# Clustered attention feeding a SoLU layer: the first batch's last pairs loaded in 3072-byte pieces, and w_out's column sums as fp32 products on PE

## The chip, the cores and the metric

The kernel runs on one core of one Trainium2 chip. A core has five engines with a queue of instructions each, taken in order: PE (TensorE, matrix products into PSUM), DVE (VectorE), ACT (ScalarE), POOL (GpSimd) and SP (SyncE, which here issues most of the transfers between HBM and the on-chip memory SBUF; 16 DMA engines carry them out). The metric is the device time of one execution in microseconds (us); lower is better.

## The reference

Attention comes first, for 4 batches, 8 heads, 768 tokens and a head dimension of 64, then a feed-forward layer over the 3072 tokens of 512 values:

```python
q_n = q / (norm(q) + 1e-6); k_n = k / (norm(k) + 1e-6); c_n = centroids / (norm(centroids) + 1e-6)
q_assign = argmax(einsum('bhsd,hcd->bhsc', q_n, c_n))          # 16 clusters a head
k_assign = argmax(einsum('bhsd,hcd->bhsc', k_n, c_n))
mask = q_assign[:, :, :, None] == k_assign[:, :, None, :]
scores = where(mask, (q @ k.T) / sqrt(64), -1e9)
attn = softmax(scores) @ v
x = attn, tokens by heads*64                                     # 3072 x 512
h = x @ w_in                                                     # 512 x 1024
solu = h * softmax(h)
ln = (solu - mean(solu)) / sqrt(var(solu) + 1e-6) * g_ln
out = ln @ w_out                                                 # 1024 x 512
```

A query sees only the keys of its own cluster. A norm of q or k does not change its argmax, so the kernel leaves it out.

## The kernel before

**Tiling.** Work goes by pairs of heads: four batches of four pairs, written (b, p), with names such as `ld0.3.1` for batch 0, pair 3, tensor 1 (0 is q, 1 is k). For each pair q and k are needed with the head dimension on the partitions. Batch 0 is loaded token by token (`load_tokens`, L353): a partition holds six tokens, and each of the two heads of the pair is a transfer of its own (192 KB, pieces of 64 fp32 values, 256 bytes, since the two heads lie side by side in SBUF). PE turns such a tile in six fp32 transposes of 128x128 (`tp`, L359) into a bank of the three-bank PSUM region `hreg`, and DVE or ACT copies it to `xt` (`xa`, L366). Pair (0,0) is done in two halves of the sequence. Batches 1 to 3 are loaded in pieces of 128 bytes and turned on DVE (`xt`, L384).

**Clusters.** From `xt` come two things. Casts (`ca`, L395) write bf16 copies into `qk`, k scaled by 1/256. A cluster group (`cl`, L407) multiplies `xt` with the centroids in fp32: four products with 32 output columns each stand side by side on PE (`tile_position`), one for each half of q and of k, over 384 tokens; the table `c_bd` has the centroids of the pair's two heads in 16 columns each, zero for the other head's rows. DVE then turns the result (`tb`), takes the maximum (`mx`), compares (`oh`) and turns it back (`ot`); four copies (`pl`, L450) place the one-hot rows below the 64 rows of q and k in `qk`, so that a score product over 80 or 96 rows adds the mask, and `bl` (L467) blanks the other head's rows for the second head.

**Attention.** `S` (L539) fills a bank of scores, two products of 256 columns in most units (one of 384 in pair (0,0), four of 128 in the last two pairs). `E` (L545) is ACT's exponential of a bank, `V` (L562) six value products of 65 columns, the last of them the sum of weights, and `N` (L587) the division on DVE. A ring of three score banks and one of nine exponential tiles tie S, E and V together. There are 294 banks: 24 of pair (0,0), 18 of every other pair.

**Feed-forward.** For each of 24 tiles of 128 tokens: x is turned by a transposing DMA (`tx`, on SP), `h` (L648) is eight products of 512 columns into hreg, then the maximum (`hm`), the exponential (`ex`, on ACT), the product (`u`), the statistics (`bn`, `ag`), another transposing DMA (`tu`), `y` (L709), eight products with w_out, and the scaling (`sc`) and store (`ou`). The mean is taken out of w_out beforehand: `sum_w_out` (`su`, L512) adds up the eight row blocks of w_out times g on DVE, one instruction a block, `me` (L521) sums that over the partitions with one fp32 product, and `ce` (L524) writes the centred bf16 weights.

**Order.** The program lists every step with its needs and then emits them in an order that is written out by hand for each engine (`ORDER`, from L28: a kind and how many of it in a row). `AWAY` (from L73) says which steps go to another engine than their usual one. A planner's costs, keys and due times stand beside each step (`add`), but the order written out decides. Since every queue is taken in order, an instruction that waits holds all that stand behind it on its engine.

The steps that the prediction speaks of are `ld` and `lo` (w_out's load) on SP, `tp`, `cl`, `S`, `V`, `me` on PE, `xa`, `ca`, the assignment steps `tb mx oh ot`, `pl`, `bl`, `N`, `su`, `ce` on DVE, and `E`, `ex` on ACT.

Of the kernel before, what the change touches and what calls it, by code (L numbers as in the profile page):

```python
# [22 lines left out]
class Weave:  # L23
# [6 lines left out]
        ld4 lv si ld11 lo lg ld lo lv ld2 lo ld3 lo ld2 lv ld3 lv ld3 li ld3 li2 ld2 li ld3 tx ld3  # L30
        lv ld3 lv ld5 tx2 lv tu ld3 tu ld lv ld9 tu ld4 lv ld6 tu2 ou2 tx lv ld3 tx ld tu ld ou lv
        tu ld6 ou ld7 tx ld5 ou ld2 lv ld2 ou ld6 ou tu ld4 tu2 lv ld pl2 tx ld2 ou ld lv2 tx lv pl
        tu2 pl tx ou2 pl3 tu2 ou tu ou tx2 tu ou tu tx tu ou tx tu ou tx ou2 tu ou tu2 ou6
    """
    ORDER["POOL"] = """
        po ca2 pl2 ca bl pl2 bl sg cv ca3 pl ca pl4 ca z bl z2 cv pl3 ca cv ca pl ca bl ca cv ca pl2
        ca pl cv pl ca cv ca cv pl2 ca wi pl wi z pl wi2 pl2 ca bl2 cv pl2 ca2 cv pl2 cv ca3 pl at z
        ca cv ca pl3 bl2 al at cv ca2 cv2 al pl ca pl ca at cv at ca3 pl3 al pl al ca6 at bl pl cv
        ca al pl3 cv2 at pl al ca2 bl ca pl2 at bl cv al pl ca at ca2 cv pl cv pl2 al pl at ca cv bl
        pl2 ca2 bl at ca3 al ca2 at cv at cv ca4 cv ca pl3 cv bl at pl al pl bl at al pl al at2 ca  # L40
        al pl cv at al2 at al3 at3 al2 at2 al2 at al2
    """
    ORDER["PE"] = """
        wm tp2 cp tp cl tp fl5 cl fl5 S3 tp S tp S2 tp2 S3 tp2 cl V tp2 V2 S3 cl S2 V3 S tp2 S2 gt
        S2 tp S2 V3 S2 tp S3 V S V S V S2 cl S3 V3 S2 V S2 V S V S4 V2 S V S2 V2 S2 V S2 me S2 V S
        V3 S2 V2 S3 cl S2 V S2 V2 S V2 S V S4 V S V3 S3 cl S3 V2 S V2 S3 V S2 V3 S2 h S h S2 h2 S3
        cl S V2 S V2 h V2 S h S2 h S h S2 V S V3 S V S V S h2 cl S2 h S h S2 V S V2 S h S2 V3 S2 y4
        S2 V2 S V2 S2 h V2 S2 h2 S2 y S V2 S y3 S3 V h2 S h S V h S V2 S2 h2 S2 V S V cl V2 S2 h V2
        S3 cl S2 V3 S2 V h S2 y S V2 S V2 S y S2 y2 h V S2 V h2 S V S h S2 h y S2 V y3 S2 V2 S h S
        V2 S V S h2 S2 V S cl h S V3 S2 h y V y S y S2 y V2 S h2 S3 V h V S y S y3 V3 h S V S2 y S y  # L50
        S2 V2 y S2 y S h V2 S2 h S V2 S2 cl S3 V2 cl h S2 V S V2 S h2 V S2 h S h S2 V cl V3 S2 V S y
        V y S3 y h S y V S V2 S2 y S V h S2 h S V2 S V2 S2 y2 S3 h2 V2 y S V2 S2 h3 S3 V h S V cl S2
        V2 S V cl S V S2 h S h V S V S y3 S2 V h V2 y S V S2 h S h S h S V2 S V S y2 h S y V2 y S V
        h S h3 S3 h V2 S2 V y S y2 V y V2 S2 h3 S3 V h y2 V y V S y V S3 h2 S V S V S y S V2 y S3 y2
        h2 S V h2 S3 h V y S V2 y3 S h S2 h V2 h S y S V2 y2 h S y S h V h S h S V S y V2 y S y S y
        h4 y4 h S h y4 S h2 V4 y3 ptx y h2 y h2 ptu2 y8 ptu2 y7
    """
    ORDER["DVE"] = """
        cn cb ca tb mx oh ot pl2 cv tb mx oh ot xa3 ca2 tb ca xa pl mx oh tb ot xa gk N su xa2 mx su
        oh xa ot N tb su3 mx N oh su3 N ot xt2 ce N ce bl xt tb mx oh ot N ce xt N ce4 tb N mx oh ot  # L60
        ce xt N xt hm tb mx u N oh ot hm xt2 u tb N mx oh hm bn2 ag bn ot N u xt bn N bn2 hm ag xt u
        bn xt hm N ag xt u tb cv bn N ag mx oh tb ot N mx hm oh N xt u bn3 hm ot bn N ag2 u bn2 xt
        ag hm N tb xt mx oh ot u N hm xt2 bn ca bn ag N xt u bn xt sc bn hm N tb mx oh ot u tb mx N
        xt hm oh tb N ot u xt mx N oh ag hm bn3 N xt u N ag ot hm xt2 tb mx u N tb oh mx hm bn2 ot u
        bn N bn2 hm oh ot ag cv ag u N bn hm bl ag u bn cv N bn cv hm bn2 u N ag sc hm bn ag bn ag N
        bn u sc hm N u ag sc bn2 hm N bn u bn ag bn ag hm N u bn ag bn hm sc u bn2 sc ag hm N bn tx
        u bn2 hm tu ag tu ag u bn2 ag sc
    """
    ORDER["ACT"] = """
        wa xa4 ca3 E6 xa E3 xa3 E78 ex E10 ex E14 ex E5 sc E6 ex E4 sc E4 ex E17 ex E sc E7 ex E6 sc  # L70
        E5 ca E3 ex E4 sc E4 ex E sc E14 ex E12 ex E7 sc E10 ex E6 sc E4 ex E9 ex E7 sc E3 ex E3 sc
        E3 ex E2 sc E5 ex E9 ex E5 ex E8 ex E sc E4 ex sc E ex E3 ex sc ex sc2 tu2 sc2 oz
# [3 lines left out]
        ca0.0.0.0.1 ca0.0.0.1.0 ca2.2.1.0 tu23.1 xa0.0.0.1 xa0.0.1.0 xa0.1.1.0 xa0.2.0.0 xa0.2.0.1  # L76
        xa0.2.1.1
    """.split(), "ACT"))
    AWAY.update(dict.fromkeys("""
        bl0.3 bl3.3 ca0.0.0.0.0 ca0.0.1.1.1 ca0.1.1.0 ca0.2.0.0 ca3.0.0.0 cv0.0.1 cv1.3.1 cv3.1.1  # L80
        cv3.2.1 cv3.3.0 pl0.0.0.0.1 pl0.0.0.1.1 pl0.0.1.0.1 sc12 sc13 sc14 sc17 sc18 sc6 tu22.0
    """.split(), "DVE"))
    AWAY.update(dict.fromkeys("""
        ca0.0.1.0.1 ca0.0.1.1.0 pl0.0.0.0.0 pl0.0.0.1.0 pl0.0.1.0.0 pl0.0.1.1.0 pl0.1.0.0 pl0.1.0.1
        pl0.1.1.0 pl0.1.1.1 pl0.2.0.0 pl0.2.0.1 pl0.2.1.0 pl0.2.1.1 pl0.3.0.0 pl0.3.0.1 pl0.3.1.0
        pl0.3.1.1 pl1.0.0.0 pl1.0.0.1 pl1.0.1.0 pl1.0.1.1 pl1.1.0.0 pl1.1.0.1 pl1.1.1.0 pl1.1.1.1
        pl1.2.0.0 pl1.2.0.1 pl1.2.1.0 pl1.2.1.1 pl1.3.0.0 pl1.3.0.1 pl1.3.1.0 pl1.3.1.1 pl2.0.0.0
        pl2.0.0.1 pl2.0.1.0 pl2.0.1.1 pl2.1.0.0 pl2.1.0.1 pl2.1.1.0 pl2.1.1.1 pl2.2.0.0 pl2.2.0.1
        pl2.2.1.0 pl2.2.1.1 pl2.3.0.0 pl2.3.0.1 pl2.3.1.0 pl2.3.1.1 pl3.0.0.0 pl3.0.1.1 pl3.1.0.0
        pl3.1.0.1 pl3.1.1.1 pl3.2.0.0 pl3.2.1.0 pl3.3.0.0 pl3.3.1.0  # L90
# [79 lines left out]
def kernel(  # L170
# [172 lines left out]
    def by_token(b):  # L343

        return b < n_turned

    def halves_of(b, p):
        return (b, p) == (0, 0)
# [9 lines left out]

    def turn_tokens(b, p, i, hf):  # L359

        j = tps[b, p, i, hf]
        for t in range(n_t // 2):
            uses(nc.tensor.transpose(hreg[:, j, t * P:(t + 1) * P],  # L363
                                     tokens(b, p, i)[:, hf * (n_t // 2) + t, :], ident_f[:]), j)
# [29 lines left out]

    def cast(b, p, i, hh, cols, e):  # L395
        xt, h = xts[b, p, i], 2 * p + hh
        r = rows(h)
        dst = side(b, p, i, hh, cols)[:D]
        if e == "ACT":
            nc.scalar.activation(dst, xt[r, cols], Act.Copy, scale=inv_C if i else 1.0)  # L400
        elif i == 0:
            VEC[e].tensor_copy(dst, xt[r, cols])  # L402
        else:
            VEC[e].tensor_scalar(dst, xt[r, cols], scalar1=inv_C, scalar2=1.0,  # L404
                                 op0=Alu.mult, op1=Alu.mult)

    def clusters(b, p, hf):  # L407
# [3 lines left out]
        for c in range(4):  # L411
# [38 lines left out]
    def place(b, p, hf, i, part, e):  # L450
# [6 lines left out]
        if e == "SP":  # L457
# [707 lines left out]
```

## Time and profile before

| | |
|---|---|
| time, median of 3 runs | 229.61 us (228.98 to 231.76) |
| profiled execution, its own time | 230.08 us |
| its span, first to last instruction | 227.7 us |
| granted TensorE clock, mean | 0.991 |
| PE busy | 218.3 us (96%), 2404 products |
| DVE busy | 198.0 us (87%) |
| ACT busy | 193.9 us (85%) |
| POOL busy | 131.4 us (58%) |
| HBM read, written | 23.11 MB, 6.29 MB |
| DMA packets | 133695, of them 124376 under 512 bytes |

The profile is of one execution, in us from its first instruction. A group line names the line of the kernel, the engine and the operation, what it writes and reads, and how often; a releaser is what ended a wait. PE's products are pipelined and their ends are modelled: a PE that is busy may still wait inside, so its work is better read from the steps between starts. The chain goes back from the last instruction to what released each step.

### The profile page before, as it was taken

The numbers are of one execution on the slowest core, as the hardware profiler recorded it, in microseconds if no ns is written. First come the engines' busy times: TensorE is split into PE (matmuls) and PEld (weight loads), VectorE is DVE, ScalarE is ACT, GpSimd is POOL, SyncE is SP. The second block draws the span as 40 slices with busy tenths as digits, with TensorE's granted clock in tenths as the row PEclk, the third lists the DMA queues.
The fourth block names the chain that finished last, engine by engine and source line by source line (L and its number), as shares of the span: only waits on it lengthen the run. The fifth ranks groups of instructions, "written<-read, shape, count | busy, mean of one in ns | idle before, by whom it ended". The sixth has DMA issues, their size and how long they took to land.

```text
span 227.7 us, 6584 instructions
## 1 busy us (share of the span) xinstructions
PE 218.3 (96%) x2404; PEld 149.1 (65%) x2404; DVE 198.0 (87%) x348; ACT 193.9 (85%) x376; POOL 131.4 (58%) x253
## 2 busy tenths in 40 slices
PE   7997999999999999999999999999999999999993
PEld 3554767666767866867667677766667676665552
DVE  2888689999999989999899997899997996988980
ACT  3776799999999999999998999999988897874462
POOL 2495596877775975598489084979542240141131
PEclk9999799999999999999999999999999999999999
DMA  6999799999999989899989999599246317557513
GB/s 154 253 227 279 158 243 210 232 192 191 189 186 164 200 132 208 194 200 217 190 143 208 181 208 166 107 199 198 53 140 124 96 32 156 137 120 210 156 69 121
DMA packets 133695, 38.95 MB, mean 171 GB/s; under 512 B 124376, under 2 KB 129184, under 8 KB 133664
## 3 DMA queue, kind: packets, MB, share of 16 engines
q1 hardware_dynamic: 131920, 38.01, 81.9%
q10 hardware_dynamic: 1744, 0.52, 0.9%
q8 instruction: 19, 0.31, 0.6%
q14 instruction: 12, 0.10, 0.1%
HBM read 23.11 MB, written 6.29 MB: 129 GB/s over the span
## 4 chain that ended last, share of the span: by engine, by line
PE 78%; DMA 5%; SPq 5%; issue 4%; ACT 4%; DVE 2%; ACTq 0%; DVEq 0%
PE sps L539 24%; PE hreg L648 18%; PE yps L709 16%; PE ops L562 13%; PE csc L413 4%; SPq L356 4%; ACT e L545 4%; DMA raw<-in_k_dram 3%; DMA out_dram<-y 1%; DMA raw<-in_q_dram 1%; PE hreg L363 1%; DVE y L726 0%; DVE nmax L654 0%; SPq L510 0%; DVE bs L676 0%
## 5 line engine op out<-in xcount | busy, mean ns | idle before, releaser
L545 ACT ACTIVATE e<-sps 128x512 bf16<-128x512 f32 (+1 forms) x294 | 151.5, 605 | 13.9 <-PE sps L539 13.0
L539 PE MATMUL sps<-qk 80*128 80x256 bf16 (+5 forms) x636 | 97.8, 265 | 1.8 <-POOL qk L460 0.4
L539 PEld LDWEIGHTS <-qk 96*128 96x128 bf16 (+1 forms) x636 | 61.2, 121 | 30.1 <-issue 10.4
L562 PEld LDWEIGHTS <-e 128*128 128x128 bf16 x1152 | 52.2, 98 | 10.3 <-issue 2.2
L562 PE MATMUL ops<-v,e 128*128 128x65 bf16 x1152 | 56.8, 194 | 0.0
L648 PE MATMUL hreg<-w_in_sb,xT 128*128 128x512 bf16 x192 | 53.1, 379 | 0.2 <-DVE xT L629 0.2
L709 PE MATMUL yps<-w_out_c,uT 128*128 128x512 bf16 x184 | 48.7, 378 | 0.0
L460 POOL COPY qk<-oht 32x384 f32<-32x384 f32 (+1 forms) x58 | 29.0, 499 | 32.2 <-DVE oht L446 24.1
L665 DVE TENSOR_TENSOR u<-e_sb,hreg 128x1024 bf16<-128x1024 bf16 x24 | 29.0, 1208 | 5.5 <-ACT e_sb L660 5.4
L660 ACT ACTIVATE e_sb<-hreg,nmax 128x1024 bf16<-128x1024 f32 x24 | 26.8, 1117 | 7.7 <-DVE nmax L654 6.0
L676 DVE BATCH_NORM_STATS2 bs<-u 128x6 f32<-128x512 bf16 x48 | 31.3, 675 | 0.2
L654 DVE TENSOR_REDUCE nmax<-hreg 128x1 f32<-128x1024 f32 x24 | 29.1, 1212 | 1.8 <-PE hreg L648 1.7
L402 POOL CAST qk<-xt 64x768 bf16<-64x768 f32 (+1 forms) x29 | 24.6, 849 | 6.1 <-ACT xt L370 3.4
L404 POOL TENSOR_SCALAR qk<-xt 64x768 bf16<-64x768 f32 (+1 forms) x30 | 25.2, 839 | 2.2 <-ACT xt L370 0.4
L709 PEld LDWEIGHTS <-uT 128*128 128x128 bf16 x200 | 17.9, 97 | 10.9
L648 PEld LDWEIGHTS <-xT 128*128 128x128 bf16 x192 | 16.8, 97 | 10.8 <-DVE xT L629 0.7
L384 DVE STREAM_TRANSPOSE xt<-raw 128x768 f32<-128x768 f32 x24 | 22.6, 956 | 0.0
L692 POOL TENSOR_SCALAR esq<-es,mv 128x1 f32<-128x1 f32 x24 | 8.2, 340 | 24.8 <-DVE mv L680 23.7
L587 DVE TENSOR_TENSOR x<-ops,den 128x384 bf16<-128x384 f32 (+1 forms) x37 | 18.6, 503 | 1.3
L478 POOL CAST v<-vf 128x384 bf16<-128x384 f32 x27 | 14.7, 549 | 4.6 <-PE ops L562 2.7
L686 POOL TENSOR_SCALAR es<-esum 128x1 f32<-128x1 f32 x24 | 5.2, 220 | 17.0 <-ACT e_sb L660 16.3
L695 POOL TENSOR_TENSOR alpha<-esq,halves 128x1 f32<-128x1 f32 x24 | 13.7, 571 | 2.0
(70 smaller groups left out, 164.7 us busy)
## 6 DMA issues: line engine op xcount, KB each, us to landing
vf<-in_v_dram SPq DMA_DIRECT2D x16, 384.0 KB, 4.6
out_dram<-y SPq DMA_DIRECT2D x23, 256.0 KB, 2.3
raw<-in_q_dram SPq DMA_DIRECT2D x50, 96.0 KB, 3.5
raw<-in_k_dram SPq DMA_DIRECT2D x50, 96.0 KB, 3.4
w_g<-in_moe_w_out_dram SPq DMA_DIRECT2D x4, 512.0 KB, 7.1
w_st<-in_moe_w_in_dram SPq DMA_DIRECT2D x4, 512.0 KB, 6.2
raw<-in_q_dram SPq DMA_DIRECT2D x6, 192.0 KB, 4.6
raw<-in_k_dram SPq DMA_DIRECT2D x6, 192.0 KB, 4.7
```

The lines of the kernel that those rows point to most:

```text
L402: VEC[e].tensor_copy(dst, xt[r, cols])
L404: VEC[e].tensor_scalar(dst, xt[r, cols], scalar1=inv_C, scalar2=1.0, op0=Alu.mult, op1=Alu.mult)
L460: ins = VEC[e].tensor_copy(dst.bitcast(F32), src.bitcast(F32).unsqueeze(1) .to_broadcast([NB, 2, n // 2]))
L539: nc.tensor.matmul(sps_[n, k][:, c0:c0 + w], side(b, h // 2, 1, h % 2, keys)[r], side(b, h // 2, 0, h % 2, slice(s0 * P, s0 * P + w))[r])
L545: nc.scalar.activation(es[n, k][:, :w], sps_[n, k][:, :w], Act.Exp, scale=exp_scale, bias=-exp_scale)
L562: nc.tensor.matmul(opss[g][:, s, :VW], es[n, k][:, c0:c0 + P], v1[slot(b, h // 2)][:, h % 2, kt, :VW], start=(kt == 0), stop=(kt == n_t - 1))
L648: uses(nc.tensor.matmul(hreg[:, at(f, f2)[1], :], xTs[f][:, dc, :], w_in_sb[:, dc, f2 * FF2:(f2 + 1) * FF2], start=(dc == 0), stop=(dc == ...
L654: uses(nc.vector.tensor_reduce(ff[f, "nmax"][:], pair_of(f), axis=AXY, op=Alu.max, negate=True), *both(f))
L660: uses(nc.scalar.activation(ff[f, "e"][:], pair_of(f), Act.Exp, bias=ff[f, "nmax"][:], accum_out=ff[f, "esum"][:]), *both(f))
L665: uses(nc.vector.tensor_tensor(ff[f, "u"][:], ff[f, "e"][:], pair_of(f), op=Alu.mult), *both(f))
L676: nc.vector.bn_stats(ff[f, "bs"][:, f2, :], ff[f, "u"][:, f2, :])
L709: ins = nc.tensor.matmul(dst, ff[f, "uT"][:, at(f, f2)[0] * (n_fc // 2) + c, :], w_out_c[:, fc, cols], start=(fc == 0), stop=(fc == n_fc - 1))
```

## The change

There are two parts, and with them the written order of every engine is new.

**Loads.** For pairs 1 to 3 of batch 0 (`twelve`), q and k of both heads come in one transfer of 384 KB: a partition holds twelve consecutive tokens of one head, 3072 bytes in a piece; the first 64 partitions are the first head, the others the second. A transpose of 128 columns then covers two tokens of 64 dimensions: after it the partitions are (parity of the token, dimension) and the columns (head, token). The copy out of PSUM (`xa`) writes every other word so that `xt` is ordered as the scores want it (`by_two`); a cast takes the tokens of one parity, for both heads, and writes every other block of 128 columns of `qk` (`every_other`); a head's scores thus need both casts of a tensor. The one-hot copies go to the same blocks and are on POOL or DVE for these pairs. A cluster group needs the centroids of one head against the rows of one parity: a table four times as wide (`c_by_two`, built by `cf` on DVE from a second transpose of the centroids, `cq`), and two products where there was one, one for each head, adding into the same bank.

**Column sums.** The eight instructions on DVE go. POOL spreads g over 32 columns for each row block (`gs`), and PE multiplies w_out's row blocks by it in fp32, four blocks side by side on PE, in two rounds (`su`); DVE or ACT copies the sums from bank 1 of hreg (`sk`), and the mean's constant is divided by 32.

**Order.** The six 384-KB loads stand ahead of all of w_out's loads on SP, one v load between them, and w_out's four follow, two after three pieces of batch 1 and two after nine. DVE has 15 casts for 5, 11 copies of turned tiles for 8, 6 one-hot copies for 3, 7 v casts for 5; POOL 46 casts for 59 and 52 one-hot copies for 58; ACT 7 casts for 4 and 5 copies of turned tiles for 8; SP 10 one-hot copies for 7. On PE the cluster groups of pairs 1, 2 and 3 stand behind 12, 18 and 31 score groups (9, 12 and 30 before), the column sums behind 37 and 40, the mean behind 47 (49), the first feed-forward product behind 79 (82).

```diff
+    def twelve(b, p):
+        return by_token(b) and not halves_of(b, p)
...
+    def load_twelve(b, p, i):
+        raws[b, p, i] = ld.tile([P, n_j, NB], F32, name="raw")
+        nc.sync.dma_start(out=raws[b, p, i][:].rearrange("p j c -> p (j c)"),
+                          in_=SRC[i][b, 2 * p:2 * p + 2].rearrange("h (q t) d -> (h q) (t d)",
+                                                                   q=D))
+    def by_two(b, p, i):
+        return xts[b, p, i][:].rearrange("p (h t n) -> p h t n", h=2, t=n_t // 2)
...
         dst, src = xts[b, p, i][:, hf * HALF:(hf + 1) * HALF], hreg[:, tps[b, p, i, hf], :HALF]
+        if twelve(b, p):
+            dst = by_two(b, p, i).rearrange("p h t (q u) -> p h t u q", u=2)[:, :, :, hf, :]
+            src = src.rearrange("p (t h q) -> p h t q", h=2, q=D)
...
+    def every_other(b, p, i, part):
+        return (qk[slot(b, p)][:, i * 2 * S:(i + 1) * 2 * S]
+                .rearrange("p (h t n) -> p h t n", h=2, t=n_t)[:, :, part::2, :])
...
+        if twelve(b, p):
+            src, dst = by_two(b, p, i)[r], every_other(b, p, i, hh)[:D]
...
+            for hh, c in ((hh, c) for hh in range(2) for c in range(4)):
+                i, part = divmod(c, 2)
+                nc.tensor.matmul(csc[c * NB:(c + 1) * NB, :], c_by_two[:, p, 2 * part + hh, :],
+                                 by_two(b, p, i)[:, hh].rearrange("p t n -> p (t n)"),
+                                 start=(hh == 0), stop=(hh == 1), tile_position=(0, c * NB))
...
+            ins = VEC[e].tensor_copy(
+                every_other(b, p, i, part)[D:D + NB].bitcast(F32),
+                src.bitcast(F32).rearrange("p (t n) -> p t n", t=n_t // 2).unsqueeze(1)
+                .to_broadcast([NB, 2, n_t // 2, P // 2]))
...
-    def sum_w_out(fc):
-        if fc == 0:
-            nc.vector.tensor_scalar(w_sum[:], w_g[:, 0, :], scalar1=g_ln2[:, 0:1], scalar2=None,
-                                    op0=Alu.mult)
-        else:
-            nc.vector.scalar_tensor_tensor(out=w_sum[:], in0=w_g[:, fc, :],
-                                           scalar=g_ln2[:, fc:fc + 1], in1=w_sum[:],
-                                           op0=Alu.mult, op1=Alu.add)
+    def spread_g():
+        nc.gpsimd.tensor_copy(g_cols, g_ln2[:].unsqueeze(2).to_broadcast([P, n_fc, NB]))
+    def sum_w_out(r):
+        for c in range(4):
+            fc = 4 * r + c
+            uses(nc.tensor.matmul(hreg[c * NB:(c + 1) * NB, 1, :], g_cols[:, fc, :], w_g[:, fc, :],
+                                  start=(r == 0), stop=(r == n_fc // 4 - 1),
+                                  tile_position=(0, c * NB)), 1)
+    def keep_sums(e):
+        src = hreg[:, 1, :]
+        uses(nc.scalar.copy(w_sum[:], src) if e == "ACT" else
+             nc.vector.tensor_copy(w_sum[:], src), 1)
...
+    nc.gpsimd.memset(own_two, 0.0)
+    for part in range(2):
+        for hh in range(2):
+            nc.gpsimd.memset(own_two[part * D:(part + 1) * D, 2 * part + hh,
+                                     hh * NC_:(hh + 1) * NC_], 1.0)
...
+    def keep_by_two():
+        nc.vector.tensor_tensor(
+            c_by_two, cs["t"][:].rearrange("p a h c -> p a (h c)").unsqueeze(2)
+            .to_broadcast([P, n_pair, 4, 2 * NC_]),
+            own_two.unsqueeze(1).to_broadcast([P, n_pair, 4, 2 * NC_]), op=Alu.mult)
...
-    add("sg", "POOL", 0.2, 20, lambda e: nc.gpsimd.memset(g_mean[:], 1.0 / d_ff))
+    add("sg", "POOL", 0.2, 20, lambda e: nc.gpsimd.memset(g_mean[:], 1.0 / (NB * d_ff)))
```

The written order of the front on PE and DVE, new (a number is how many in a row):

```diff
-        wm tp2 cp tp cl tp fl5 cl fl5 S3 tp S tp S2 tp2 S3 tp2 cl V tp2 V2 S3 cl S2 V3 S tp2 S2 gt
+        wm tp2 cp tp cl tp fl5 cl fl5 S3 cq tp S tp S2 tp S tp S2 tp2 S2 V S V2 cl S V S V2 tp S tp2
+        S3 cl S2 V2 S V S tp S2 tp S tp S2 V3 S gt S3 cl S2 V3 S V S V S V S su S3 su S3 V4 S2 V2 S2
...
-        cn cb ca tb mx oh ot pl2 cv tb mx oh ot xa3 ca2 tb ca xa pl mx oh tb ot xa gk N su xa2 mx su
+        cn ca cb ca3 tb mx oh ot pl2 tb mx oh ot xa3 ca pl xa cf xa ca xa tb mx xa2 oh N ot tb pl2
+        bl xa2 cv xa N gk mx xt oh ot ca pl N ca xt ca tb mx sk cv oh N xt ce ot cv tb mx oh ot N ca
```

More of the change, by code (lines that the diff above doesn't have):

```diff
@@ L805 @@
     add("cb", "DVE", 0.27, -500, lambda e: keep_centroids(), ["cp"], give="m")
+    add("cq", "PE", 0.28, 0, lambda e: turn_centroids(), ["cn"], ["cp"], take="m")
+    add("cf", "DVE", 0.65, -490, lambda e: keep_by_two(), ["cq"], give="m")
     def before(idx, back):
@@ L907 @@
             old = last[-3] if len(last) >= 3 else None
-            add(f"cl{t}", "PE", 0.72 - 0.22 * hf if half else 0.87, first - 9,
-                (lambda e, b=b, p=p, hf=hf: clusters(b, p, hf)), kept + ["cb"], take="m")
+            add(f"cl{t}", "PE", (0.72 - 0.22 * hf if half else 1.45 if twelve(b, p) else 0.87), first - 9,
+                (lambda e, b=b, p=p, hf=hf: clusters(b, p, hf)), kept + ["cf" if twelve(b, p) else "cb"], take="m")
             add(f"tb{t}", "DVE", 0.37 if half else 0.56, first - 20,
@@ L948 @@
             else:
[L949 removed]
+                nd |= {f"ca{b}.{p}.{x}.{y}" for x in range(2)
+                       for y in (range(2) if twelve(b, p) else (hh,))}
                 ts = (f"{b}.{p}",) * 2
@@ L1119, with ring_free @@
             also={"DVE": 0.62})
-    for fc in range(n_fc):
-        add(f"su{fc}", "DVE", 0.78 if fc else 0.5, 30 + fc, (lambda e, fc=fc: sum_w_out(fc)),
-            [f"lo{fc // 2}"] + ([f"su{fc - 1}"] if fc else ["gk"]))
-    add("me", "PE", 0.9, 36, lambda e: mean_w_out(), [f"su{n_fc - 1}", "sg"] + [
-        x for j, x in enumerate(ring_h[-3:], len(ring_h) - 3) if j % 3 == 2], last_tp[-1:])
+    def ring_free(bank):
+        return [x for j, x in enumerate(ring_h[-3:], len(ring_h) - 3) if j % 3 == bank]
+    add("gs", "POOL", 0.35, 20, lambda e: spread_g(), ["gk"])
+    for r in range(n_fc // 4):
+        add(f"su{r}", "PE", 1.06, 30 + r, (lambda e, r=r: sum_w_out(r)),
+            ["gs", f"lo{2 * r}", f"lo{2 * r + 1}"] + ring_free(1),
+            last_tp[-1:] + [f"su{x}" for x in range(r)])
+    add("sk", "DVE", 0.6, 34, keep_sums, [f"su{n_fc // 4 - 1}"], also={"ACT": 0.48})
+    add("me", "PE", 0.9, 36, lambda e: mean_w_out(), ["sk", "sg"] + ring_free(2), last_tp[-1:])
     for fc in range(n_fc):
```

134 lines of the change are left out of this document (68 added, 66 removed).

## The prediction

> **What bounds the kernel now.** I read the page's chain first: PE carries most of it, so a change counts only through PE's idle time and PE's work. A busy PE is modelled, so I price PE's work by the steps from start to start in the chain: 4 score products of 256 columns 0.44 us (0.11 each), 18 value products 0.57 (0.032 each), a feed-forward product of 512 columns 0.216, one cluster group ("csc") 0.78, the fp32 mean product 0.94.
>
> ```profile
> PE 78%; DMA 5%; SPq 5%; issue 4%; ACT 4%; DVE 2%; ACTq 0%; DVEq 0%
> ...
> 28.18 0.78 PE csc L413 x8
> ...
> 37.80 0.94 PE hreg L522 x2
> 38.74 0.44 PE sps L539 x4
> ...
> 39.59 0.57 PE ops L562 x18
> ```
>
> By these prices the whole queue holds about 203 us of work plus 4.1 of warm-up products. From 80 to 100 us the counts by line (61 scores, 120 values, 22 + 14 feed-forward, 2 cluster groups) give 6.7 + 3.8 + 7.8 + 1.6 = 19.9 of 20 us: PE is full there, and stays so to the end. From 20 to 60 us the same sum is 31 of 40. So time is to be had, or PE work to be hidden, only before about 57 us.
>
> Three stages lie there. Up to 26 us the front waits. The timeline of PE shows the stop: it has nothing from 20.5 to 21.9, held by the last K load, and the next products are slow, because the granted clock fell (windows).
>
> ```profile
> 19.86 0.65 PE L539 MATMUL sps<-qk 80*128 80x384 bf16 x2
> 21.91 0.78 PE L363 MATMUL hreg<-ident_f,raw 128*128 128x128 f32 x3 [1.40 <-DMA raw<-in_k_dram]
> ```
>
> ```profile
> 15.00:20.00 5.00, 5.00 (x61) 3.36 (x61) 4.90 (x10) 3.45 (x8) 2.59 (x5) 1.00 1.16 299
> 20.00:25.00 5.00, 3.60 (x29) 2.45 (x28) 3.88 (x9) 2.47 (x7) 3.78 (x10) 0.70 0.86 233
> ```
>
> (Columns: window, length, busy of PE, weight loads, DVE, ACT, POOL, then clock, DMA share, GB/s.) From 29 to 58 us ACT sets the pace: 19 exponentials in 9.46 us, 0.498 each, hardly a gap between groups, while a bank costs PE 0.22 + 0.13 = 0.35.
>
> ```profile
> 25.79 3.43 ACT L545 ACTIVATE e<-sps 128x384 bf16<-128x384 f32 x7 [0.24 <-PE sps L539]
> 29.38 9.46 ACT L545 ACTIVATE e<-sps 128x512 bf16<-128x512 f32 x19 [0.16 <-PE sps L539]
> 39.05 4.03 ACT L545 ACTIVATE e<-sps 128x512 bf16<-128x512 f32 x8 [0.22 <-PE sps L539]
> ```
>
> From 58 us, when the feed-forward products have joined, PE is the bound. What the front saves by then is therefore saved at the end, unless PE's work after it grows.
>
> **The loads.** The DMA view of the first 30 us, in 40 slices of 0.75 us, shows two levels: 212 to 222 GB/s while the 256-byte pieces of pairs 1 to 3 run, 313 to 378 when w_out's 2-KB rows do.
>
> ```profile
> GB/s 0 0 104 227 219 252 248 240 351 278 214 249 219 221 220 212 220 219 222 214 222 224 313 333 312 335 378 350 229 92 126 305 289 172 198 39 13 79 319 303
> ```
>
> The six tiles are 2.36 MB: 10.8 us at 218 GB/s, 7.1 at 330. Unknown is only where in 218 to 350 the 3072-byte pieces lie; I take 330, the w_out rows, the nearest long ones. Counted from 7.2 us, where v's first load ends, with 0.39 MB of v between, the last K tile lands near 15.5 us instead of 21.8; no w_out load stands ahead of it on SP any more. The stop at 20.5 and the low clock behind it go. At 218 GB/s it lands near 20, still in time for the last transposes.
>
> **What PE gets.** Each of three cluster groups has 16 passes for 8: 3 x 0.78 = 2.34. Two column-sum groups of 512 columns: 0.78 x 512/384 = 1.04 each, 2.08 (floor 0.94, the mean product; four in a row, 3.76, would deny what the csc row shows). A second centroid transpose 0.27. Sum 4.7 us, all before 35 us. A score group right behind a cluster group takes 0.57 instead of 0.44 (chain, at 67.54); two more such changes are 0.26, inside my rounding.
>
> **What DVE gets.** Gone: w_out's sums, 7.0 + 0.5 us. Added by the new order: 7 full casts at 0.69 to 1.07 (0.85) = 5.9, 3 half casts 1.2, 3 copies out of PSUM 1.6, 3 one-hot copies 1.3, 2 v casts 0.9, the wide centroid table 0.7 (384 columns from PSUM cost 0.557), the sums' copy 0.55, a blank 0.4, one more scaling 0.7: 13.2. DVE ends 5.7 us up, not down; the order spends the room on POOL's work.
>
> **The other queues.** POOL loses 13 casts (0.86 each) and gets the spread of g (128x256; between a 0.21 fill and a 1.04 cast, I take 0.41, the row of a blank) and five fills at the start, 0.21 + 4 x 0.105 = 0.63. These stand ahead of the centroids' root, for which POOL waits 0.9 anyway. SP loses six loads and takes ten one-hot placements for seven; each waits there for its one-hot with loads and transposes queued behind it (in the old order two such waits were 6.1 us together, and PE's own waits do not show them). I cost these at nothing; if a load of a later batch came late by one such wait, it would be 3 us once.
>
> **The walk along the new queues.** (1) Three more half casts stand before the first one-hot; beside the wait for ACT's copy that costs 0.4: first scores 9.87, not 9.43. (2) 24 exponentials at 0.42 follow; the cluster groups of pairs 1 and 2, now 1.56 long, leave ACT without scores about 1.1 and 0.8 us; DVE's row of copies, casts and one-hot steps ends pair 1's one-hot near 20.7, its placing near 22.4, so pair 1's first exponential is at 23.5. Before, it was at 26.3 (the second of the group at 25.79). Gain 2.8. (3) The next 18 exponentials take in one more cast on ACT (0.84), and PE, from score group 30 to 46, has 1.56 + 2.08 + 0.94 + 16 x 0.22 + 12 x 0.19 = 10.4 us in 8 us of exponentials; three banks of lead and the cast cover all but 0.8. Gain left: 2.8 - 0.84 - 0.8 = 1.2. (4) DVE from 11.1 us to the blank of pair 3: 11 copies 5.5, casts 4.4, the assignment steps 8.4, five normalisations 3.6, four transposes 3.6, the rest 5.3, sum 30.8, plus about a microsecond of waits: 43. Pair 3's second head needs it near 43.5. It just holds, where the old order had some 3 us over (42.97 against 46.2). (5) From there the queues are alike: first feed-forward product behind 79 score groups (82 before), first feed-forward exponential behind 87 in both. The 4.7 us of PE work have gone into idle time; 1.2 us of the front remain.
>
> The profiled execution took 230.08 (span 227.7), 0.47 over the median 229.61. 230.08 - 1.2 = 228.9 on its scale, **228.4** against the median.
>
> **Unknown prices.** The copies out of PSUM now write every other fp32 word. No row has such a pattern; nearest is the same copy in one piece, 0.54; twice that, 1.08, is the other end. I take 0.54, the only row of this copy. [...] Casts and one-hot copies go in blocks of 128 or 64 words: the plain rows (0.69 to 1.07 on DVE, 0.86 and 0.51 on POOL), up to half more.
>
> **Rivals.**
> *DVE's queue is late* (slower). Its place is step 4. If the strided copy costs 1.08, eleven of them add 5.9 us; 0.5 us is over, so pair 3 waits 5.4: 228.4 + 5.4 = 233.8. At half that surcharge, 228.4 + 2.45 = 230.9. It decides from 0.15 us more a copy (1.7 us in all: the 0.5 and the 1.2). For it: DVE is 97% busy from 30 to 60 us (windows). Against it: the trace has plain reads from PSUM at 0.54, and no sign that writing limits them.
>
> *DVE and POOL in each other's way.* POOL's cast takes 0.82 alone (39.92) but 1.29 and 1.16 beside w_out's sums (29.82, 32.08), and a sum 0.74 alone, 0.98 to 1.15 then. Taking the sums off DVE ends this; the five full casts that DVE has before pair 3's blank may bring it back, 5 x 0.4 = 2.0 us on a queue that has 0.5 over: 228.4 + 1.5 = 229.9. The rows agree that two such instructions stretch each other where DVE's has two tensors of SBUF; none settles it for casts. [...]
>
> *PE's additions are not hidden.* If step 3 costs all that it exceeds (2.4 us, and the 0.84) and step 2 saves only the stop of 1.4 and 0.5 of slow clock: 229.6 - 1.9 + 3.2 = 230.9.
>
> *The loads were never the point*: if the pieces run at 218 GB/s and DVE's row alone sets pair 1 (its one-hot is later than before, 20.7 against 19.5), step 2 gives 1 and step 3 takes 1.6: 230.2.
>
> *More is gained*: DVE's casts run at their short end (0.69), and step 3 costs nothing for the PE lead: 2.8 to 4 us, 225.6 to 226.8.
>
> **Chances.** Forecast 0.42; more gained 0.16; additions not hidden 0.12; loads not the point 0.12; the lock 0.08; DVE late 0.10 (half of it over 2%). Two per cent, about what a measurement of this kernel can tell from no change, is 225.0 to 234.2: faster 0.05, same 0.87, slower 0.08. Range 225.2 to 232.6: it takes in the rivals but the worst of the late DVE queue and the best of the gain.
>
> **What would show it.** Right: no PE wait on K near 21 us, clock 1.00 there, loads of 384 KB that land by 16 us, the first 512-wide exponential near 23.5, cluster groups of 1.56, column sums of 1.04, first feed-forward exponential near 57.7 instead of 58.9. Wrong: strided copies well over 0.6, exponentials from 30 to 48 us with gaps on one-hot copies or blanks, DVE's one-hot steps of pair 3 after 41, or a PE that is less than full after 60 us, which no step here allows for.

## The result, and the profile after

The changed kernel takes **230.63 us** (median of 9 runs, 229.41 to 231.57), the kernel before 229.3 us beside it (9 runs, 227.22 to 231.76). The ratio is **1.0087, 95% interval 1.0059 to 1.0114**: about 2.0 us slower (1.4 to 2.6). The ratio leaves a disturbed run of before out; the two medians alone give 1.0058. Forecast were 228.4 us, 1.2 less than before, in a range from 225.2 to 232.6.

The profiled execution of the changed kernel took 231.02 us, with a span of 229.2 and a mean clock of 1.000. First the views that the prediction named. The windows (window, length, busy of PE, weight loads, DVE, ACT, POOL, then clock, DMA share, GB/s):

```profile
15.00:20.00 5.00, 4.68 (x57) 2.90 (x61) 4.90 (x11) 3.29 (x9) 3.47 (x5) 1.00 0.75 199
20.00:25.00 5.00, 5.00 (x72) 3.65 (x64) 4.82 (x10) 4.65 (x12) 3.09 (x5) 1.00 1.04 208
```

Between 20 and 25 us PE is now busy all the time, with 72 products for 29, and the clock is 1.00 for 0.70. The loads, in the DMA view of the first 30 us (40 slices of 0.75 us), and in the page's list of DMA issues:

```profile
GB/s 0 0 105 224 231 263 231 211 320 340 369 332 373 397 397 397 416 404 323 211 138 27 120 396 205 243 319 265 203 165 164 206 147 377 361 362 288 290 356 315
```

```profile
raw<-in_q_dram SPq DMA_DIRECT2D x3, 384.0 KB, 6.5
raw<-in_k_dram SPq DMA_DIRECT2D x3, 384.0 KB, 6.8
```

From slice 8 to 18 (6 to 14 us) 320 to 416 GB/s run where before had 212 to 351. The last K tile of pair 3 lands at 15.73 us (forecast 15.5; 21.8 before). The prices of the work that was added on PE, in its timeline:

```profile
15.31 1.50 PE L439 MATMUL csc<-xt,w_out_c 128*32 128x384 f32 x16 [0.41 <-DVE w_out_c L852]
...
30.12 1.06 PE L556 MATMUL hreg<-w_g,w_out_c 128*32 128x512 f32 x8
```

A cluster group takes 1.50 (forecast 1.56). One of the two rounds of column sums, four products of two passes each, takes 1.06 (forecast 1.04). The timeline of ACT, to be read beside the three lines of the prediction:

```profile
21.23 5.96 ACT L589 ACTIVATE e<-sps 128x384 bf16<-128x384 f32 x13 [0.35 <-PE sps L583]
...
33.36 15.72 ACT L589 ACTIVATE e<-sps 128x512 bf16<-128x512 f32 x31 [0.18 <-PE sps L583]
...
57.78 1.11 ACT L704 ACTIVATE e_sb<-hreg,nmax 128x1024 bf16<-128x1024 f32 x1
```

The first exponential of pair 1 starts at 23.56 (in the group at 21.23; forecast 23.5), the first feed-forward exponential at 57.78 (forecast 57.7; 58.9 before). So at these two marks the trace does what was forecast, to 0.1 us. Against the one profile from which the forecast was made, the rest of the queue loses the lead again. The largest piece is one stop of PE, and three timelines show it (PE, POOL, SP's own):

```profile
124.76 0.40 PE L583 MATMUL sps<-qk 80*128 80x256 bf16 x2 [1.57 <-issue]
```

```profile
124.78 0.59 POOL L505 MEMSET qk<- 16x384 f32 x1 [1.58 <-DMA qk<-oht]
```

```profile
119.40 0.52 SPq L393 DMA_DIRECT2D raw<-in_k_dram  x1
120.03 0.47 SPq L780 DMA_DIRECT2D out_dram<-y  x1
120.59 0.63 SPq L494 DMA_DIRECT2D qk<-oht  x1
```

The last line is a one-hot placement (`pl2.2.1.0`), one of the ten that the new order gives to SP. DVE had finished its one-hot at 116.2 (`ot`, the transpose that starts at 115.65), but SP reached it only at 120.59, behind loads and a store. The transfer landed at 124.67, 4.1 us after its issue, where 2.0 is the median of these placements; POOL's blank and PE's scores waited for it. From start to start of its products, less their own time, PE lost 1.73 us.

The chain that ended last, on the page, shows the same from afar:

```profile
PE 63%; DVE 15%; DMA 8%; issue 5%; ACT 4%; POOL 3%; SPq 1%; DVEq 0%; ACTq 0%; POOLq 0%
```

PE's share fell from 78% to 63%, and DVE's rose from 2% to 15%. Some of this is the way by which the chain reaches the stop. But in order of time the chain also runs over DVE later, near the end of the third batch:

```profile
174.69 0.60 DVE bs L720
176.06 1.15 DVE bs L720 x2
177.21 1.13 DVE u L709
```

The next table follows single instructions through the traces (us from the span's start; exponentials counted from 0, so number 24 is the first of pair 1). "Before, second" is a second profile of the unchanged kernel, from the run before_again below.

| | before | before, second | after | placed_on_pool | half_clusters |
|---|---|---|---|---|---|
| exponential 24 | 26.18 | 23.77 | 23.56 | 23.19 | 23.36 |
| exponential 60 | 44.69 | 42.23 | 43.49 | 43.13 | 43.50 |
| exponential 184 | 123.96 | 121.96 | 122.88 | 122.42 | 122.68 |
| exponential 194 | 130.38 | 128.39 | 131.56 | 129.40 | 129.67 |
| last product of PE | 223.83 | 221.74 | 225.79 | 224.04 | 223.25 |
| span | 227.7 | 225.6 | 229.2 | 227.6 | 226.7 |

Against the first profile of before, the changed kernel leads by 1.2 us at exponential 60 and by 1.1 at number 184, trails by 1.2 ten exponentials later, and by 2.0 at PE's last product. Against the second it leads by 0.2 at exponential 24 and is 1.3 behind already at number 60, long before the stop. The second profile is of a quick execution (228.03 us, the median of its runs is 229.21), so the usual one lies between the two profiles.

### The profile page after: what moved, and what is told of

Its sections match the earlier page's. It is cut to its first block, busy times and chain, and to the rows that moved or that the text cites. A ratio compares the mean times of both kernels' runs of the same rounds, so it can differ in the third digit from the quotient of the medians.

```text
span 229.2 us, 6662 instructions
## 1 busy us (share of the span) xinstructions
PE 220.0 (96%) x2445; PEld 148.0 (65%) x2445; DVE 201.5 (88%) x361; ACT 196.4 (86%) x376; POOL 117.4 (51%) x237
## 4 chain that ended last, share of the span: by engine, by line
PE 63%; DVE 15%; DMA 8%; issue 5%; ACT 4%; POOL 3%; SPq 1%; DVEq 0%; ACTq 0%; POOLq 0%
PE sps L583 19%; PE hreg L692 13%; PE yps L753 11%; PE ops L606 10%; PE csc L444 3%; ACT e L589 3%; DMA raw<-in_k_dram 3%; DVE u L709 3%; DMA xT<-x 2%; DVE bs L720 2%; DVE nmax L698 2%; PE csc L439 2%; DMA out_dram<-y 2%; DMA uT<-u 1%; PE hreg L377 1%
## 5 line engine op out<-in xcount | busy, mean ns | idle before, releaser
L583 PE MATMUL sps<-qk 80*128 80x256 bf16 (+5 forms) x636 | 95.1, 264 | 3.0 <-issue 1.6
L583 PEld LDWEIGHTS <-qk 96*128 96x128 bf16 (+1 forms) x636 | 60.0, 121 | 29.7 <-issue 12.0
L606 PEld LDWEIGHTS <-e 128*128 128x128 bf16 x1152 | 49.8, 97 | 11.7 <-issue 2.7
L606 PE MATMUL ops<-v,e 128*128 128x65 bf16 x1152 | 54.2, 193 | 0.2
L692 PE MATMUL hreg<-w_in_sb,xT 128*128 128x512 bf16 x192 | 52.1, 379 | 0.2
L496 POOL COPY qk<-oht 32x384 f32<-32x384 f32 (+1 forms) x43 | 21.0, 488 | 21.6 <-DVE oht L477 13.7
L429 POOL TENSOR_SCALAR qk<-xt 64x768 bf16<-64x768 f32 x26 | 22.2, 854 | 2.8 <-DVE xt L387 1.3
L427 POOL CAST qk<-xt 64x768 bf16<-64x768 f32 x20 | 16.6, 830 | 4.0 <-DVE xt L387 2.3
L514 POOL CAST v<-vf 128x384 bf16<-128x384 f32 x25 | 12.9, 531 | 10.1 <-DMA vf<-in_v_dram 9.4
L768 ACT ACTIVATE y<-yps,alpha 128x512 f32<-128x512 f32 x16 | 11.1, 692 | 4.7 <-PE yps L753 3.3
```

The source lines that it names most:

```text
L429: VEC[e].tensor_scalar(dst, src, scalar1=inv_C, scalar2=1.0, op0=Alu.mult, op1=Alu.mult)
L496: ins = VEC[e].tensor_copy(dst.bitcast(F32), src.bitcast(F32).unsqueeze(1) .to_broadcast([NB, 2, n // 2]))
L583: nc.tensor.matmul(sps_[n, k][:, c0:c0 + w], side(b, h // 2, 1, h % 2, keys)[r], side(b, h // 2, 0, h % 2, slice(s0 * P, s0 * P + w))[r])
L606: nc.tensor.matmul(opss[g][:, s, :VW], es[n, k][:, c0:c0 + P], v1[slot(b, h // 2)][:, h % 2, kt, :VW], start=(kt == 0), stop=(kt == n_t - 1))
L692: uses(nc.tensor.matmul(hreg[:, at(f, f2)[1], :], xTs[f][:, dc, :], w_in_sb[:, dc, f2 * FF2:(f2 + 1) * FF2], start=(dc == 0), stop=(dc == ...
```

## The experiments

The first four runs weigh two causes of the loss: the placements on SP, that is, the new order; and PE's added work, which the prediction had put into idle time. A third came up with them: that there was never as much to save in the front as the first profile shows. Ratios are to the kernel before, timed on the same chip beside each (35 runs a set; 229.3 us is taken where a ratio is turned into us). A difference of two ratios is uncertain by about 0.004, 0.9 us, by their intervals.

### placed_on_pool, no_sp_placing_b12

```diff
 # placed_on_pool: the one placement of the stop leaves SP's queue for POOL's
-ORDER["SP"]:    ... ld9 ou pl lv ld10 ...
+ORDER["SP"]:    ... ld9 ou lv ld10 ...
-ORDER["POOL"]:  ... bl pl ca al2 pl ca3 ...
+ORDER["POOL"]:  ... bl pl ca al2 pl2 ca3 ...
 # no_sp_placing_b12: so do the other four placements of batches 1 and 2
```

> One step of the changed kernel is moved: the placing of pair (2,2)'s first one-hot rows for k goes from a transfer in SP's queue to POOL, beside its sister copy. In the changed kernel PE stands 1.73 us at 123 us and POOL's blank waits for that transfer until 124.8. Theory A, the gain of the front is lost again at this late transfer: 1.6 us less than the changed kernel, ratio to the kernel before 1.002 instead of 1.0087. Theory B, the 4.5 us of added PE work set the time and the stop only moves the waiting about: no more than 0.3 us less, 1.0075 or more.

> All five one-hot placings of batches 1 and 2 that the changed kernel issues on SP go to POOL; those of batch 3 stay. Theory A: the 1.6 us of the run with one moved placing, and up to 0.4 more where loads stood behind a placing; ratio 0.999 to 1.003. Theory B: as the changed kernel, 1.0075 or more. If POOL's five more copies (2.5 us) hold its casts, it is worse than the run with one moved.

Measured: 229.91 us, ratio 1.0059 (1.0028 to 1.0090), and 229.46 us, 1.0058 (1.0032 to 1.0085). The window from 120 to 130 us, of the changed kernel and then of placed_on_pool:

```profile
120.00:130.00 10.00, 8.43 (x86) 5.63 (x85) 7.73 (x15) 8.36 (x17) 4.01 (x10) 1.00 0.94 187
```

```profile
120.00:130.00 10.00, 9.89 (x114) 7.21 (x115) 9.33 (x16) 9.90 (x20) 3.88 (x10) 1.00 0.99 188
```

PE has 9.89 us of work in ten for 8.43, ACT 9.90 for 8.36. The stop is gone, and 0.0028 of the ratio with it (0.65 us), less than the 1.73 of the trace and between the two theories. The profile of half_clusters below, which kept this placement on SP, has no such stop either:

```profile
120.00:130.00 10.00, 9.89 (x111) 7.10 (x112) 9.29 (x16) 9.90 (x20) 3.43 (x9) 1.00 0.91 180
```

There SP reached the placement at 120.11, behind the same loads and store and as long after its one-hot (4.4 us). It landed 2.2 us after its issue, and PE went on at 122.86 without a stop. In the changed kernel a landing of 2.2 us would have come at 122.8, when PE asked for it at 123.0. So the late place in the queue used up the slack, and the slow landing made the stop. How many executions of the changed kernel have it is not known. The other four placements cost nothing more that these runs show.

What the placement costs in the median is not shown. The intervals of these two runs and of the change overlap. The edit of no_sp_placing_b12 on top of half_clusters (below) gives 0.0036, about the same, but the medians, each less that of before beside it, give 1.33 us for the change and 1.26 for placed_on_pool, next to no gain.

### half_clusters

```diff
-for hh, c in ((hh, c) for hh in range(2) for c in range(4)):
+for c in range(4):
     i, part = divmod(c, 2)
-    nc.tensor.matmul(csc[...], c_by_two[:, p, 2 * part + hh, :], by_two(b, p, i)[:, hh]...,
-                     start=(hh == 0), stop=(hh == 1), tile_position=(0, c * NB))
+    nc.tensor.matmul(csc[...], c_bd[:, p, :], by_two(b, p, i)[:, part]...,
+                     tile_position=(0, c * NB))
```

> The changed kernel with 8 passes instead of 16 in the cluster groups of pairs 1 to 3: one product for both heads with the narrow centroid table over the tokens of one head, so that the clusters of these pairs are not the reference's; everything else stays. PE has 2.3 us less work. Theory A (the front has idle time for PE's additions): 0.3 to 0.8 us less than the changed kernel, ratio 1.005 to 1.0075, with the late transfer still there. Theory B (PE's work sets the time): 2.3 us less, ratio 0.999.

Measured: 228.61 us, ratio 1.0032 (1.0006 to 1.0058): 0.0055, or 1.25 us (0.4 to 2.1 by the two intervals), off the change for 2.3 us less on PE before 35 us, between the two theories. By step 3 of the prediction PE's work there went into idle time but for 0.8 us.

### sums_alone

```diff
 # the kernel before and its order; w_out's column sums on PE
-DVE:  su0 ... su7        (one multiply-add over 128x512 each)
+PE:   su0 su1            (four products side by side each, behind score groups 37 and 40)
+DVE:  sk                 (the copy of the sums);   POOL:  gs   (g spread)
```

> The kernel before with the column sums on PE alone: old loads, old clusters, the old order but for the moved steps (column sums behind score groups 37 and 40 on PE, their copy on DVE behind pair 3's comparison, g's spread on POOL). PE has 2.1 us more, DVE 7 less between 21 and 38 us. Theory A: within 0.3% of the kernel before, 0.998 to 1.003, since DVE had 3 us over and ACT sets the pace there; some 0.5 us of exponentials wait behind the column sums. Theory B: 2.1 us more, 1.009.

Measured: 228.96 us, ratio 1.0034 (1.0004 to 1.0065), about 0.8 us slower (0.1 to 1.5), though DVE lost 7 us of work; that is just outside theory A and well short of theory B. Its trace held a surprise: the loads are those of the kernel before, in the same order, and yet there was no stop for K and no slow clock.

```profile
20.00:25.00 5.00, 4.92 (x60) 3.52 (x60) 4.38 (x12) 4.97 (x13) 4.58 (x12) 1.00 1.14 276
```

So the stop that the change was to take away did not belong to the loads alone. The next run therefore takes a second profile of the kernel before.

### before_again

The kernel before, unchanged.

> The kernel before, unchanged, for a second profile. The theory that the stop of 1.40 us on the last K tile and the clock of 0.70 behind it belong to the one profiled execution of before: PE has no wait for a K load at 20 to 22 us, the clock is 1.00 in that window, the 24th exponential (the first of pair 1) comes near 23.5 and not at 26.2, the span is 226 to 226.5, the time 1.000 of before. The rival, that the stop is in every execution and the prediction's step 2 stands: the 24th exponential again near 26.2, the clock near 0.70, the span near 227.5.

Measured: 229.21 us, ratio 0.9992 (0.9961 to 1.0024), as it must be. The profiled execution has a span of 225.6. PE's waits, the window and PE's timeline at the place of the stop:

```profile
PE hreg L363 <- DMA raw<-in_k_dram: 0.6, 2, 0.4
```

```profile
20.00:25.00 5.00, 4.55 (x59) 3.33 (x59) 4.70 (x11) 4.59 (x12) 3.54 (x9) 1.00 1.08 259
```

```profile
21.02 0.52 PE L363 MATMUL hreg<-ident_f,raw 128*128 128x128 f32 x3 [0.43 <-DMA raw<-in_k_dram]
```

(Waits: us in total, times, longest; window from 14 to 24 us.) The wait of 1.40 us is one of 0.43 here, the products behind it take 0.52 for three and not 0.78, and exponential 24 comes at 23.77, 2.41 before the first profile. Nearly all of this lead is kept: 2.1 us at PE's last product. So **the first profile's front was that of a late execution**. The median span of before lies between the two, at 226.2 to 227.05 in the three sets. The slow clock is rarer still: each run records its mean granted clock, and of the 105 runs of before in these sets four lie under 0.995 (the first profile: 0.991).

### late_k, late_k_in_3072

```diff
 # the last K load of pair 3 goes one place back on SP, behind the second load of w_out
-ORDER["SP"]:  ... lo lg ld lo lv ...
+ORDER["SP"]:  ... lo lg lo ld lv ...
```

The first is the kernel before with this edit, the second the kernel with the 3072-byte loads alone.

> The kernel before, where the last K load of pair 3 is issued on SP one place later, behind the second 512-KB load of w_out. This makes the stop of the first profile in every execution. If such a stop is worth what the prediction's step 2 gave it: PE waits for K 1.4 us or more near 21 us, the 24th exponential comes at 25.5 to 27 (23.77 in the second profile of before), the span is 1.5 to 2.5 us longer, ratio 1.006 to 1.011. The rival, that later idle time takes the stop in: 1.000 to 1.003. If the stop also lowers the granted clock, as in the first profile, the window from 20 to 25 us shows under 0.9; if that fall had another cause, 1.00.

> The same place later for the last K load, in the kernel with the 3072-byte loads alone, where it lands about 6 us before it is needed. No wait of PE for K over 0.5 us, the 24th exponential near 24.0 as in the run of the loads alone, ratio 0.996 to 1.000 (loads alone 0.998). If it costs as much as in the kernel before, 1.005 or more, the loads buy no slack.

Measured: late_k 230.84 us, ratio 1.0065 (1.0035 to 1.0095); late_k_in_3072 228.54 us, 0.9983 (0.9948 to 1.0018). PE's waits and the windows of late_k:

```profile
PE hreg L363 <- DMA raw<-in_k_dram: 2.4, 1, 2.4
```

```profile
20.00:25.00 5.00, 2.61 (x30) 1.96 (x29) 3.29 (x7) 2.61 (x7) 3.52 (x9) 0.93 0.99 241
25.00:30.00 5.00, 5.00 (x51) 3.35 (x49) 2.83 (x8) 4.29 (x9) 3.11 (x6) 0.73 0.72 163
```

This is the picture of the first profile, made on purpose: a stop of 2.4 us, and the clock falls behind it, here about 4 us after the stop begins and 1.5 after it ends (so the window from 20 to 25 us still has 0.93, where under 0.9 was expected). Exponential 24 comes at 26.09, the trace ends at 223.82 (last product), both as in the first profile. Seven of its twelve runs have a mean clock of 0.993 or less. So such a stop, with the slow clock behind it, costs about 1.5 us (0.8 to 2.2), at the low end of what was expected for it. What step 2 had wrong is how often it is there. With the 3072-byte loads the same delay costs nothing: no wait for K in PE's list, exponential 24 at 23.84.

### loads_alone, both_old_order

```diff
 # loads_alone: the kernel before and its order, with load_twelve, by_two, every_other,
 #              16 passes in cl of pairs 1 to 3, and the second centroid transpose
-SP:   si ld11 lo ...          +SP:   si ld5 lo ...
+PE:   cq behind S0.2          +DVE:  cf behind xa0.1.1.1
 # both_old_order: this and the edit of sums_alone
```

> The kernel before with the 3072-byte loads alone, and with them what they bring (16 passes in three cluster groups, a second centroid transpose, strided copies), in the old order; w_out's sums stay on DVE. PE gets 2.6 us. If nothing is to be had in the front of a usual execution and PE's work counts: ratio 1.004 to 1.010, the span 1 to 2 us over before's 226.2. If the loads take away a stop that every execution has: ratio 0.990 to 0.997.

> Both parts of the change in the old order, with the fewest moves; the change's own new order is left out. If the loss is PE's added work, 1.007 to 1.011, the same as the change (1.0087) or the sum of the two parts alone. If the new order of the queues loses it (the placements on SP above all): 1.003 or less.

Measured: loads_alone 228.97 us, ratio **0.9979** (0.9954 to 1.0004); both_old_order 230.06 us, 1.0032 (1.0000 to 1.0064). The windows of before_again and of loads_alone, for the speed of the loads:

```profile
10.00:15.00 5.00, 4.93 (x41) 3.10 (x39) 4.39 (x10) 4.69 (x12) 3.81 (x9) 1.00 1.00 219
```

```profile
10.00:15.00 5.00, 4.81 (x43) 3.22 (x41) 4.66 (x10) 4.76 (x12) 3.80 (x10) 1.00 1.04 401
```

219 GB/s become 401. The loads pay for the 2.6 us that they add on PE, and perhaps a little more; neither outcome that was expected (1.004 to 1.010, or 0.990 to 0.997) came. The two parts together in the old order stand 0.0055 under the change, near the outcome that was expected if the new order loses it. So the rest of the change's loss, about 1.3 us, is most likely in its new order; the two intervals still overlap by a little (up to 1.0064, and from 1.0059).

### doubled_clusters

```diff
-for c in range(4):
+for c in [c for c in range(4) for _ in range(2 if b == 0 and p else 1)]:
```

> The kernel before, where each of the cluster passes of pairs 1 to 3 is made twice: 2.3 us more on PE before 35 us, and nothing else. If PE's added work before 57 us goes into idle time, as the prediction has it: ratio 1.000 to 1.002. If it counts in full: 2.3 us, ratio 1.008 to 1.011. Between the two, the share that is hidden is read off.

Measured: 230.28 us, ratio 1.0033 (1.0000 to 1.0066): 0.76 us (0 to 1.5) for 2.34 us of added products, about a third. By half_clusters it was 1.25 of 2.3, about a half. That run excludes that PE's work before 57 us is free, this one that it is paid in full; the share between is known only roughly.

### half_clusters_no_sp

The edits of half_clusters and no_sp_placing_b12 together.

> The changed kernel with both earlier edits: 8 passes for 16 in the three cluster groups, with a table over one head's tokens (so the clusters of pairs 1 to 3 are not the reference's), and the five placements of batches 1 and 2 on POOL for SP. If PE's added work and the placements on SP are two separate parts of the loss: 1.0087 less 0.0055 less 0.0029, ratio 1.000. If they share a part: 1.002 to 1.004.

Measured: 229.24 us, ratio **0.9996** (0.9969 to 1.0024). Within the interval the two parts add up: 1.0087 - 0.0055 - 0.0029 = 1.0003. With the doubled cluster work and the five placements out, nothing of the loss is left; by the ledger below, the loads' gain then makes up for the column sums and for what else the new order costs.

### ff_product_later

```diff
-PE:  ... S70.1 h12.0.0 h12.0.1 V68.0 V68.1 y8.3 S70.2 V69.0 ...
+PE:  ... S70.1 V68.0 V68.1 y8.3 S70.2 h12.0.0 h12.0.1 V69.0 ...
```

> The kernel with the 3072-byte loads alone, and the first two feed-forward products of block 12 moved behind two value groups, an output product and a score group on PE, about 1 us. In the profiles of this order PE waits 0.7 to 1.3 us there (near 148 us) for the transposed x. If that wait is in every execution: it goes, the span is 0.5 to 1 us under that of the loads alone, ratio 0.993 to 0.996, faster than before. If it only moves to the next product: 0.998.

Measured: 228.59 us, ratio 0.9986 (0.9954 to 1.0018), the same as the loads alone: no gain shown. PE's waits in the traces, first of loads_alone, then of sums_alone:

```profile
PE hreg L686 <- DMA xT<-x: 0.7, 1, 0.7
```

```profile
PE hreg L693 <- DMA xT<-x: 1.3, 1, 1.3
```

In the trace with the products moved this wait is not in the list any more, but the time did not follow, so either the wait is not in most executions or its place is taken by others. Its profiled execution shows something else, a K load of pair (0,0) that came late at 8 us (timeline of PE):

```profile
8.03 0.90 PE L378 MATMUL hreg<-ident_f,raw 128*128 128x128 f32 x3 [0.98 <-DMA raw<-in_k_dram]
```

The clock then read 0.51 from 8 to 10 us, and the first exponential came at 11.99 for 9.98 in loads_alone. This one load, which no 3072-byte piece replaces, lost about 2 us in this execution (230.91 us; the median of its runs is 228.59).

Three kernels with the 3072-byte loads alone (loads_alone, late_k_in_3072, ff_product_later) thus stand at 0.998 to 0.999. That is the best version of these runs; each interval reaches 1, so it is not shown to be faster than before.

## Why the prediction was wrong, point by point

**Right, as mechanisms and as prices.** The piece size: 330 GB/s was taken, 320 to 416 came (401 from 10 to 15 us in loads_alone), and no K tile of pairs 1 to 3 was waited for. Cluster groups 1.50 for 1.56, column sums 1.06 for 1.04. Step 2: pair 1's first exponential at 23.56 for 23.5. Step 3: the lead of 2.6 us over the first profile at exponential 24 is 1.2 at number 60, as forecast. Step 4: the blank of pair 3 ends at 43.44 for 43, and its second head's scores start at 44.24 without a wait. DVE's busy time rose by 3.5 us, not 5.7. The first feed-forward exponential at 57.78 for 57.7. Step 1 was 0.4 too late (first scores at 9.44 for 9.87). The strided copies out of PSUM cost 0.558 us in the median (0.542 with plain ones in sums_alone), so the rival of a late DVE queue has no ground. Its price came by the nearest row, 0.54.

**Wrong: step 5** ("From there the queues are alike", which gave the 1.2 us to the end), and the sentence on SP's placements ("I cost these at nothing"). The new order was put at nothing; by both_old_order against the change it costs about 1.3 us. In the trace a lead of 1.1 us at exponential 184 became a lag of 1.2 at number 194, by the stop behind a placement on SP, 1.73 us of PE. That is one execution, as the stop for K was in the first profile of before; taking the placement away is worth 0.65 us in the ratios, which is not clear of their noise. The prediction saw the ten placements, and it saw that each waits in SP's queue; it asked what a waiting placement does to the loads behind it, and not what the loads and stores ahead of it do to the placement, which is issued 4.4 us after its one-hot is ready and so has no slack left for a slow landing. "What would show it" did name the sign: a PE that is less than full after 60 us.

**Wrong in size: step 2, the gain of 2.8 us.** It was read off one execution, whose total lay only 0.47 above the median, and this was taken as a sign that its front was usual. Against the second profile pair 1's first exponential comes 0.2 us earlier (23.56 for 23.77), not 2.6. What the loads save in the median follows from loads_alone and the price of PE's work: 0.5 us gained, and 2.6 us of added products paid, at a third to a half (0.9 to 1.4 us): 1.4 to 1.9 us. This is an estimate from these runs, with half a us of noise each way; no run shows the gain by itself.

**About right in size: step 3**, but spread over both parts. It took 1.6 us for PE's additions and a cast; the runs show 0.8 for the sums and 0.8 to 1.25 for the clusters.

The ledger, in us, from the ratios of the runs:

| | forecast | runs |
|---|---|---|
| the loads' gain (step 2) | -2.8 | -1.4 to -1.9 |
| PE's added work (step 3) | +1.6 | +1.6 to +2.0 |
| both, in the old order | -1.2 | +0.7 (0 to 1.5) |
| the new order (step 5, SP) | 0 | +1.3 (0.3 to 2.2), of it the placement +0.65, not clear of noise |
| the change | -1.2 | +2.0 (1.4 to 2.6) |

The first two rows give -0.3 to +0.6, the run of both parts 0.7 with its wide interval. Of the new order's 1.3 us some 0.65 are named. What the rest is stays open: from exponential 194 to PE's last product the changed kernel takes 94.2 us and placed_on_pool 94.6, the old order 93.4 in both profiles of before; the orders differ there, so the two can't be compared piece by piece. The chain names DVE at 174 to 178 us, where PE's products then stand 0.3 us apart twice instead of 0.06; its other stops in that stretch are 0.6 us or less, and no run took them apart.

Among the rivals, "PE's additions are not hidden" (230.9) came nearest the time (230.63), and its premise that step 2 saves little was right in the median; that of step 3 costing all was not, and it had no new order in it, so its number is in part luck. DVE and POOL in each other's way (called the lock among the chances; no run shows a lock) and the late DVE queue are not what lost the time: POOL's cast at 30.13 us took 0.82 in the changed kernel, as alone, with a normalisation and a cast of DVE beside it, and the blank of pair 3 came 0.4 us after its forecast and was waited for by nobody.

## What to carry to other kernels

A gain that is read off a stop in one profiled execution is worth its price times its frequency: look for the stop in a second profile, or in the recorded clocks and spans of the runs, before it is put into a sum; that the total is near the median says nothing of a single stage. The same holds for a stop in the profile after: here its removal gave less than half of what the trace shows, if anything. A transfer that other engines wait for, and that stands in a queue with bulk loads and stores, can be issued late by what lies ahead of it (here 4.4 us after its one-hot), so its slack is to be counted at both ends, with the landing at its longest and not at its median (here 4.1 us in the stop, 2.0 in the median). PE's work in a stage that shows idle time need be neither free nor paid in full: here about a third to a half of it came through.

## What the runs showed of the hardware

- **Clock.** In the first profile of before, a wait of 1.40 us on a PE that had been busy for 9.5 of the 10 us from 10 to 20 was followed by half clock from 22.03 to 25.45 us, 3.41 us long; the wait of 2.4 in late_k by half clock about 4 us after its start (0.64, 0.50, 0.50 and 0.66 in the four microseconds from 24, some 3.40 us in all); that of 0.98 at 8 us in ff_product_later by half clock till about 11.5 (0.51 from 8 to 10, then 0.50 and 0.77, some 3.42 us). The stop of 1.57 at 123 us of the changed kernel was followed by none (1.00 in every microsecond from 122 to 130). So the length of the stop alone does not decide. The clock records of the first profile of before show full clock for 17.07 us, half for 3.41 and full for 201.39, that of the changed kernel full clock for 225.28: 5, 1, 59 and 66 times 3.413. So in these two traces the clock changes at marks 3.41 us apart. In the last 3.41 us before the fall PE is idle for 1.40 us in before, about 1.9 in late_k and about 1.5 in ff_product_later. In the changed kernel a mark at 124.46 cuts the stop (123.19 to 124.76), and the stretch before it holds 1.27 us. Whether the idle time of a stretch is what decides, these runs do not show.
- **A placement's landing.** A one-hot placement from SBUF to SBUF by SP lands 2.0 us after its issue in the median of the nine that the changed kernel's trace follows. Three are slower: 3.8, 4.1 (the one of the stop) and 4.9 us.
- **Time outside the span.** What lies between span and time is 2.41 us in the median of before, 2.43 with the doubled clusters, 2.35 in late_k, but 2.10 with the loads alone and 1.8 in the changed kernel and with the sums alone. So the changed kernel's span grew by some 0.6 us more than its time did. Why is not known.
